# The small sums of A22 on VectorE behind the gates, and a wider order of the streams

## The chip, the cores and the metric

The kernel runs on one core of a Trainium2 chip. The metric is the device time of one execution in microseconds; the profiler's span of an execution goes from its first to its last instruction. TensorE does the matrix products, VectorE (DVE), ScalarE (ACT) and GpSimd (POOL) do the elementwise work, and SyncE (SP) issues most of the DMAs.

## The reference

A causal convolution of 7 taps per head over a sequence, with softmaxed weights, then a two-layer block with hardswish:

```python
out = np.einsum('hk,bskhg->bshg', softmax(weight), x_unf)     # x: 8 x 4096 x 192, 7 taps
x = out.reshape(32768, 192)
h = x @ w_in                                                  # 192 x 2048
g = h * np.clip(h + 3.0, 0.0, 6.0) / 6.0
return g @ w_out                                              # 2048 x 192
```

## The kernel before, in words

The tokens are worked through in 32 blocks of 1024, two halves of 512. The first block is done apart. For each of the blocks 1 to 31 the loop at the end of the kernel calls `first_layer` and then `second_layer`.

**First layer.** It has 16 units; `NP` is 8. Unit n multiplies one chunk of `w_in` (128 rows of the 2048) with the convolved block in three passes of exact float parts (18 matmuls, L437), into two banks of PSUM. Then `relu` (ACT, L311) and `gate` (VectorE, L315) make 128x1024 values of g. Gate n reads PSUM and the relu's result. Units 0 to 7 give the quarters A11 and A22 of g, units 8 to 15 the quarters A21 and A12. Four pairs of banks are used in turn, so unit n + 4 needs gate n to have read its banks. Behind the units stand other jobs: convolution taps of the next block on VectorE (L903; at n = 1, 5 and 9), sums for the second layer (`small_sums` on POOL for n below 8, L527; `g_sums`, L385, for S3 = A11 - A21 in pairs of chunks behind n = 9, 11, 13 and 15), and DMAs issued by POOL that add A22 onto A21 in place, which makes S1 (L506).

**Second layer.** The product with `w_out` is done as a 2x2 block product with 7 multiplications in place of 8 (Winograd's form). The sums S1 to S4 of g and T1 to T4 of the weights go into products 1 to 7. Three of the products (1, 4 and 5) have their last third of output columns done by the same scheme once more, on halves and quarters. These need small sums: `s1` for product 1, `s5` for product 5, and z1 to z4 of A22 for product 4:

z1 = x21 + x22, z2 = z1 - x11, z3 = x11 - x21, z4 = x12 - z2, where x11 to x22 are the quarters of A22.

TensorE's columns are used as four groups of 32, so four streams of matmuls run side by side. `plain`, `plain_half` and `small4` put matmuls into a stream; each has a place on a clock counted in units of 256 columns, and all four streams are 81 units long. `do(t, job)` puts a job of another engine at time t of that clock. All of it is sorted by clock and then recorded, and each engine runs its own instructions in that order. Partial sums wander from one stream's rows to another's by copies on ACT (L564), for example A4 to B4, B4 to C4, or e of one stream to e of the next; a VectorE sum (L405) takes some out into `p1` and `p4`.

The six banks are taken from units 12, 13 and 14 of the first layer: d and e from 12, b and c from 13, a and x_ from 14. `A4`, `E4`, `B4` and `C4` are parts of bank d; product 4's third output part `t4` is in b, product 1's third in b's fourth rows (V).

**What makes z1 to z4 before.** `s4_sums` in `first_layer`: ACT writes a seed, a copy of one quarter with a sign (L477), behind units 7 to 10; POOL then issues a DMA that adds another tensor onto it (`onto`, L480). z2 takes z1 and z4 takes z2 by such DMAs, so the third waits for the first, and the fourth for the third. In POOL's queue they stand between the S3 sums and the S1 DMAs. z3, z4 and their weights carry the opposite sign (`small_weights` with sign -1, and a fifth weight tile -b22).

**The last stage of a block.** `between` places the rounding of the next block's convolved values into high and low parts (`split_high` on ACT, L420; `split_rest` on VectorE, L423), the DMAs that swap their halves (`swap_parts`, SP), and the next load. The small sums s5 and the sums S2 and S4 (both `g_sums` with 4 chunks at a time) are on VectorE.

Of the kernel before, what the change touches and what calls it, by code (L numbers as in the profile page):

```python
# [31 lines left out]
def kernel(  # L32
# [30 lines left out]
    QS = 32  # L63
# [63 lines left out]
    w_out = cst.tile([P, NP, 7, DH], F32, name="w_out")  # L127
    B11, B12, B21, B22, T1, T2, T4 = range(7)
    T3 = B12
    w_s = cst.tile([P, 2, 4, NP // 2, QS], F32, name="w_s")  # L130
    w_s4 = cst.tile([P, 5, NP // 2, QS], F32, name="w_s4")

    w_in_bits = moe_w_in.bitcast(U32).rearrange("(p s) (c f w) -> c p s f w", s=K3, f=P, w=2)
    w_out_bits = moe_w_out.bitcast(U32).rearrange("(k c p) w -> p c k w", p=P, k=2)
# [240 lines left out]
    def g_sums(engine, which, slots, width):  # L375

        forms = {
            3: (S3, A11, A21, ALU.subtract),
            2: (S2, S1, A11, ALU.subtract), 4: (S3, A12, S2, ALU.subtract),
        }  # L380
        for n in which:
            o, a, b, op = forms[n]
            for p in slots[::width]:
                r = slice(p, p + width)
                engine.tensor_tensor(out=o[:, r], in0=a[:, r], in1=b[:, r], op=op)  # L385
# [18 lines left out]
    def add(out, x, y, op=ALU.add):  # L404
        nc.vector.tensor_tensor(out=out, in0=x, in1=y, op=op)  # L405
# [42 lines left out]
    def sums_a22():  # L448

        early = [  # L450
            part[:].rearrange("p s n -> p (s n)")[:, : NP * TH // 2]
            .rearrange("p (u t) -> p u t", t=TH)
            for part in z_early or y_own
        ]
        return early + [z[:, k] for k in range(2)]

    def first_layer(i, jobs):

        def unit(n):
            slot = free_slots.pop(0)  # L460
            for m_ in range(3):
                for s in range(K3):
                    products(n, slot, s, (m_,), s == 0, s == K3 - 1)
            to, both = places(n, slot)
            relu(to, both)
            gate(to, both)
            free_slots.append(slot)

        count = 2 * NP
        x11, x12, x21, x22 = four_parts(A22)  # L470

        def begin_sums():
            z_early[:] = own_tiles("z")
            seed(0, x21, 1.0)

        def seed(k, x, sign):
            nc.scalar.mul(sums_a22()[k], x, sign)  # L477

        def onto(k, x):
            nc.gpsimd.dma_start(out=sums_a22()[k], in_=x, accum_op=ALU.add)  # L480


        s4_sums = {
            NP - 1: [lambda: seed(2, x11, -1.0)],
            NP: [begin_sums, lambda: onto(2, x21), lambda: onto(0, x22)],
            NP + 1: [lambda: seed(1, x11, -1.0)],
            NP + 2: [lambda: seed(3, x12, -1.0), lambda: onto(1, sums_a22()[0])],
            NP + 6: [lambda: onto(3, sums_a22()[1])],
        }
        for job in jobs.get(-1, ()):  # L490
            job()
        for n in range(count):
            unit(n)
            for job in jobs.get(n, ()):
                job()
            for job in s4_sums.get(n, ()):
                job()
            if n == 1:
                s1.append(ot.tile([P, NP, N], F32, name="s1", tag="shared")[:])
            if n < NP and n % 2:  # L500
                small_sums(s1[-1], A11, (1, 2, 3, 4), nc.gpsimd, every[n - 1 : n + 1])
            if n > NP and n % 2:
                pair = slice(n - NP - 1, n - NP + 1)
                g_sums(nc.vector if n in (NP + 3, count - 1) else nc.gpsimd, (3,), range(NP)[pair], 2)
                if n + 3 < count:
                    nc.gpsimd.dma_start(out=S1[:, pair], in_=A22[:, pair], accum_op=ALU.add)  # L506
        for pair in (slice(NP - 2, NP), slice(NP - 4, NP - 2)):
            add(S1[:, pair], A21[:, pair], A22[:, pair])
# [4 lines left out]
    def four_parts(x):  # L513
        return [x[:, c::2, t] for t in halves for c in range(2)]
# [11 lines left out]
            o, p, q, op = forms[n]  # L526
            engine.tensor_tensor(out=o, in0=p, in1=q, op=op)  # L527

    def small_weights(to, w, sign=1):

        b11, b12, b21, b22 = (
            w_out[:, c::2, w, q * QS : (q + 1) * QS] for c in range(2) for q in range(2)
        )
        t1, t2, t3, t4 = (to[:, n] for n in range(4))
        third_sum = (t3, b22, b12) if sign > 0 else (t3, b12, b22)
        for o, p, q in ((t1, b12, b11), (t2, b22, t1), third_sum, (t4, b21, t2)):
            nc.gpsimd.tensor_tensor(out=o, in0=p, in1=q, op=ALU.subtract)
        if sign < 0:
            nc.scalar.mul(to[:, 4], b22, -1.0)

    def second_layer(i, between):
        last = i + 1 == NB
# [20 lines left out]
        def do(t, fn, *args, **kw):  # L563
            streams[3].append((t - 0.5, lambda: fn(*args, **kw)))  # L564
# [23 lines left out]
        def small(n, m_, out, start=False, j=3):  # L588

            x, w = prod[n]  # L590
            x11, x12, x21, x22 = four_parts(x)
            b11, b12, b21, b22 = (
                w_out[:, h::2, w, q * QS : (q + 1) * QS] for h in range(2) for q in range(2)
            )
            if n == 4:
                z1, z2, z3, z4 = sums_a22()
                t1, t2, t3, t4, b22 = (w_s4[:, k] for k in range(5))
            else:
                sums, ws = (s1[-1], w_s[:, 0]) if n == 1 else (s5, w_s[:, 1])
                z1, z2, z3, z4 = four_parts(sums)  # L600
                t1, t2, t3, t4 = (ws[:, k] for k in range(4))
            xm, wm = {
                1: (x11, b11), 2: (x12, b21), 3: (z4, b22), 4: (x22, t4),
                5: (z1, t1), 6: (z2, t2), 7: (z3, t3),
            }[m_]
            for u in range(NP // 2):
                put(j, 1, lambda u=u: matmul(
                    j, out[:, lo], wm[:, u], xm[:, u], start and u == 0
                ))
# [25 lines left out]
            do(clock[q], copy, out=e[rows(q + 1)] if q < 2 else p1[third], in_=e[rows(q)])  # L635

        plain(0, t4, 4, 2, (0,), True)
        plain_half(0, t4, 4, 2, 1, 0)
        do(clock[0], copy, out=t4[second], in_=t4[first])
        small4(0, 1, d[first], True)  # L640
        do(clock[0], copy, out=B4, in_=A4)
        small4(0, 2, d[first])
        do(clock[0], copy, out=p4[first, lo], in_=A4)
        plain_e(0)
        small4(0, 5, d[first, TH:], True)
        do(clock[0], copy, out=p4[second, lo], in_=E4)
        plain(0, c, 7, 0, every, True)

        plain(1, c, 7, 1, every[:3], True)
        for t, chunks in ((0, (2, 3, 4)), (1, (1, 2, 3, 4))):  # L650
            for ch in chunks:
                plain_half(1, t4, 4, 2, ch, t)
        do(clock[1], copy, out=t4[third], in_=t4[second])
        small4(1, 6, d[second])
        do(clock[1], copy, out=C4, in_=B4)
        plain_e(1)
        plain(1, c, 7, 1, every[3:6])
        small4(1, 3, d[second])
        do(clock[1] + 1, add, p4[second, lo], B4, p4[second, lo])
        plain(1, c, 7, 1, every[6:])  # L660

        plain(2, c, 7, 2, every, True)
        plain(2, t4, 4, 2, (5, 6, 7))
        do(clock[2], copy, out=p4[third], in_=t4[third])
        small4(2, 7, d[third])
        do(clock[2], add, p4[second, hi], C4, p4[second, lo])
        plain_e(2)
        plain(2, a, 2, 2, every[:2], True)
        small4(2, 4, d[third])
        do(clock[2], copy, out=p4[first, hi], in_=C4)  # L670
        plain(2, a, 2, 2, every[2:6])

        for q in range(NQ):
            if q < 2:
# [54 lines left out]

        for t, job in between:  # L730
            do(t, job)
        for t, n in ((22.3, 1), (30.7, 2), (30.7, 3)):
            do(t, small_sums, s5, S1, (n,), nc.vector)
        do(31, tiles)
        do(33, lambda: copy(out=late["p7"], in_=c[m]))
        do(37, copy, out=b[m], in_=p1[:])
        do(37, g_sums, nc.vector, (2,), every, 4)
        do(37, small_sums, s5, S1, (4,), nc.vector)
        do(37, g_sums, nc.vector, (4,), every, 4)
        do(61, lambda: add(late["u3"], b[m], late["p7"]))  # L740
        do(61, lambda: add(late["p7"], late["u3"], p4[:]))
        do(61, lambda: store(i, late["p7"], 1, 0))
# [69 lines left out]
    with tc.manual_schedule():  # L812
# [158 lines left out]

        def begin_block_two():
            w_sums(((T1, B12, B11), (T2, B22, T1), (T4, B21, T2)))
            for n, w in enumerate((B11, T1)):
                small_weights(w_s[:, n], w)
            small_weights(w_s4, T4, -1)
            conv.extend(conv_jobs(2))
            for job in conv[:3]:
                job()
# [20 lines left out]
        for i in range(1, NB):  # L1000
            jobs = {4 * n + 1: [job] for n, job in enumerate(conv[4:])}
            jobs[-1] = left + conv[3:4]
            first_layer(i, jobs)
            conv = []

            def begin_conv():
                x_tiles[i + 2] = load_x(i + 2)
                conv.extend(conv_jobs(i + 2))

            between = []  # L1010
            if i + 1 < NB:
                between = [(18, split_high), (20, split_rest), (23, swap_parts)]
            if i + 2 < NB:
                between += [(20, begin_conv), (60, lambda: conv[0]()), (72, lambda: conv[1]()), (73, lambda: conv[2]())]
            left = second_layer(i, between)
# [33 lines left out]
```

## Time and profile before

| | us |
|---|---|
| three runs | 2433.25, 2437.59, 2437.73 |
| median | 2437.59 |
| the profiled execution | 2436.49 |
| its span | 2434.7 |
| one steady block (1302.72 to 1378.04) | 75.32 |
| its first layer, units 0 to 7 and 8 to 15 | 16.90 and 16.43 |
| its second layer, to 1354.13 and after | 18.08 and 23.91 |

The columns of a timeline are start, length, engine, line, operation, output and inputs with their sizes, and a count where equal instructions were merged; brackets give the engine's idle time before the row and what ended it. A row of the chain of waits has start, length, engine, and what was worked on. The granted clock of TensorE was 0.997 of full speed over the whole span.

### The profile page before, as it was taken

Reading aid. Unit: us, or ns where it says so; the run is one execution under the profiler, and the core shown is the slowest. Engines: PE = TensorE matmul, PEld = TensorE weight load, DVE = VectorE, ACT = ScalarE, POOL = GpSimd, SP = SyncE. Lnnn points to the kernel's source line nnn. Section 1 sums busy time; section 2 is a strip of 40 time slices with the busy share of each in tenths; the row PEclk is TensorE's granted clock in tenths of the full one; section 3 lists DMA queues with packets and bytes.
Section 4 is the critical chain, followed back from the end, with each engine's and each line's share of the span. In section 5 each row is a group of like instructions: output and inputs, shape, how many; then the busy total and the mean of one; then the engine's idle time right before and its main releaser. Section 6 shows DMA issues by size and latency. Waiting matters only on the chain.

```text
span 2434.7 us, 52196 instructions
## 1 busy us (share of the span) xinstructions
PE 2330.1 (96%) x22652; PEld 1553.6 (64%) x22652; DVE 1959.7 (80%) x1681; ACT 1159.8 (48%) x1545; POOL 846.3 (35%) x803
## 2 busy tenths in 40 slices
PE   9999999999999999999999999999999999999998
PEld 5556666666675666766667656676566666666666
DVE  8877788887887888888878878788887878878866
ACT  7435545345443454434554445444455443454534
POOL 4513443134431344322443224432144332344323
PEclk9999999999999999999999999999999999999999
DMA  6355543455434554345543354533545435554344
GB/s 156 59 100 94 103 71 58 95 98 99 79 61 84 98 98 79 66 80 100 97 85 72 67 104 93 92 71 62 105 92 102 69 58 100 97 100 71 60 81 66
DMA packets 290774, 208.12 MB, mean 85 GB/s; under 512 B 209104, under 2 KB 245968, under 8 KB 290544
## 3 DMA queue, kind: packets, MB, share of 16 engines
q0 software_dynamic: 58912, 98.65, 24.9%
q1 hardware_dynamic: 230392, 105.86, 20.7%
q8 instruction: 177, 2.90, 0.5%
q14 instruction: 53, 0.43, 0.1%
q10 hardware_dynamic: 1240, 0.27, 0.1%
HBM read 31.72 MB, written 25.17 MB: 23 GB/s over the span
## 4 chain that ended last, share of the span: by engine, by line
PE 64%; POOL 13%; DMA 12%; ACT 5%; issue 3%; DVE 2%; POOLq 0%; ACTq 0%; DVEq 0%
PE psum L567 40%; PE psum L437 22%; DMA z<-g 12%; POOL s L527 7%; POOL s L385 3%; POOL z L480 2%; PE psum L326 2%; ACT psum L564 2%; POOL g L506 1%; ACT y L420 1%; DVE g L315 1%; ACT g L311 1%; DVE p L405 1%; ACT p L564 0%; ACT p L705 0%
## 5 line engine op out<-in xcount | busy, mean ns | idle before, releaser
L567 PE MATMUL psum<-g,w_out 128*32 128x512 f32 (+1 forms) x6526 | 1073.2, 519 | 40.6 <-ACT psum L564 40.6
L311 ACT ACTIVATE g<-psum,half 128x1024 f32<-128x1024 f32 x512 | 572.2, 1118 | 393.5 <-PE psum L437 393.3
L315 DVE SCALAR_TENSOR_TENSOR g<-g,psum 128x1024 f32<-128x1024 f32 x512 | 618.3, 1217 | 173.5 <-ACT g L311 169.3
L567 PE MATMUL psum<-s,w_out 128*32 128x256 f32 (+1 forms) x3272 | 717.2, 574 | 40.6 <-POOL s L385 40.6
L527 POOL TENSOR_TENSOR s<-g 128x256 f32<-128x256 f32 x248 | 267.5, 1079 | 1261.6 <-DVE g L315 969.0
L567 PEld LDWEIGHTS psum<-g,w_out 128*32 128x32 f32 x6526 | 395.2, 110 | 341.1 <-ACT psum L564 139.9
L437 PE MATMUL psum<-y,w_in 64*128 64x512 f32 x4608 | 548.4, 393 | 0.2
L437 PE MATMUL psum<-y_other,w_in 64*128 64x512 f32 x4608 | 530.1, 386 | 0.1
L437 PEld LDWEIGHTS psum<-y,w_in 64*128 64x128 f32 x4608 | 428.0, 184 | 134.9 <-issue 26.0
L437 PEld LDWEIGHTS psum<-y_other,w_in 64*128 64x128 f32 x4608 | 431.7, 184 | 92.7 <-DMA y_other<-y 0.5
L903 DVE SCALAR_TENSOR_TENSOR y<-x,c_sb,y 128x1536 f32<-128x1536 f32 x186 | 334.9, 1800 | 2.9 <-ACT y L901 1.8
L567 PEld LDWEIGHTS psum<-s,w_out 128*32 128x32 f32 x3272 | 231.6, 110 | 126.8 <-POOL s L385 54.6
L567 PE MATMUL psum<-g,w_s 128*32 128x256 f32 x1488 | 283.5, 379 | 0.0
L385 DVE TENSOR_TENSOR s<-g 128x1024 f32<-128x1024 f32 (+1 forms) x124 | 267.1, 2175 | 2.1
L385 POOL TENSOR_TENSOR s<-g 128x1024 f32<-128x1024 f32 x62 | 206.4, 3330 | 0.0
L564 ACT COPY psum<-psum 32x512 f32<-32x512 f32 (+1 forms) x217 | 106.3, 490 | 202.9 <-PE psum L567 200.5
L567 PE MATMUL psum<-z,w_s 128*32 128x256 f32 x992 | 178.8, 383 | 16.2 <-DVE p L405 16.0
L423 DVE TENSOR_TENSOR y<-y,y 128x1536 fp32r<-128x1536 f32 (+1 forms) x33 | 55.9, 1694 | 168.5 <-ACT y L420 168.5
L567 PE MATMUL psum<-s,w_s 128*32 128x256 f32 x744 | 181.5, 382 | 0.0
L567 PEld LDWEIGHTS psum<-g,w_s 128*32 128x32 f32 x1488 | 144.5, 110 | 50.4
L527 DVE TENSOR_TENSOR g<-g 128x1024 f32<-128x1024 f32 x124 | 148.6, 1219 | 5.4 <-PE psum L567 4.5
L385 DVE TENSOR_TENSOR g<-g 128x2048 f32<-128x2048 f32 x62 | 139.3, 2288 | 1.0
(94 smaller groups left out, 1627.4 us busy)
## 6 DMA issues: line engine op xcount, KB each, us to landing
y_other<-y SPq DMA_DIRECT2D x124, 384.0 KB, 5.7
z<-g POOLq DMA_DIRECT2D x62, 512.0 KB, 7.8
g<-g POOLq DMA_DIRECT2D x62, 512.0 KB, 8.1
z<-z POOLq DMA_DIRECT2D x62, 512.0 KB, 5.2
out_dram<-results SPq DMA_DIRECT2D x378, 64.0 KB, 2.0
x<-in_x_dram SPq DMA_DIRECT2D x53, 388.5 KB, 9.5
g<-in_moe_w_in_dram SPq DMA_DIRECT2D x16, 192.0 KB, 6.1
stage<-in_moe_w_out_dram SPq DMA_DIRECT2D x8, 384.0 KB, 6.2
```

The lines of the kernel that those rows point to most:

```text
L311: nc.scalar.activation(r6, h, ACT.Relu, bias=half[:], scale=1.0 / 6.0)
L315: nc.vector.scalar_tensor_tensor(out=g_, in0=g_, scalar=1.0, in1=h, op0=ALU.min, op1=ALU.mult)
L326: lambda p=p: nc.tensor.matmul(out=bank[j * QS : (j + 1) * QS, tokens], lhsT=w_out[:, p, w, cols], rhs=x[:, p, tokens], start=(first and p ...
L385: engine.tensor_tensor(out=o[:, r], in0=a[:, r], in1=b[:, r], op=op)
L405: nc.vector.tensor_tensor(out=out, in0=x, in1=y, op=op)
L423: engine.tensor_tensor(out=r32(out), in0=x, in1=high, op=ALU.subtract)
L437: nc.tensor.matmul(out=psum[:, 2 * slot + k], lhsT=r32(w_in_parts[wn][r, c, s]), rhs=r32(y_other[r, yn, s] if group else y_own[yn][r, s]), ...
L480: nc.gpsimd.dma_start(out=sums_a22()[k], in_=x, accum_op=ALU.add)
L527: engine.tensor_tensor(out=o, in0=p, in1=q, op=op)
L564: streams[3].append((t - 0.5, lambda: fn(*args, **kw)))
L567: nc.tensor.matmul(out=out, lhsT=w, rhs=x, start=start, stop=True, tile_position=(0, j * QS), skip_group_check=True,)
L903: jobs.append(lambda k=k: nc.vector.scalar_tensor_tensor(out=y[:], in0=x[:, :, k : k + N], scalar=c_sb[:, k : k + 1], in1=y[:], op0=ALU.mu ...
```

## The change

z1 to z4 are made by VectorE (`a22_sum`): each of the four sums is cut into two calls of two of the four chunks, and one call stands behind each of the units 8 to 15, in the order z1, z3, z2, z4. The ACT seeds and the four DMAs per block are gone, with the opposite signs. The S3 pair behind unit 11 goes from VectorE to POOL. In the second layer the streams are put in another order, and the jobs of other engines at other places on the clock.

```diff
         def begin_sums():
             z_early[:] = own_tiles("z")
-            seed(0, x21, 1.0)
-        def seed(k, x, sign):
-            nc.scalar.mul(sums_a22()[k], x, sign)
-        def onto(k, x):
-            nc.gpsimd.dma_start(out=sums_a22()[k], in_=x, accum_op=ALU.add)
-        s4_sums = {
-            NP - 1: [lambda: seed(2, x11, -1.0)],
-            NP: [begin_sums, lambda: onto(2, x21), lambda: onto(0, x22)],
-            NP + 1: [lambda: seed(1, x11, -1.0)],
-            NP + 2: [lambda: seed(3, x12, -1.0), lambda: onto(1, sums_a22()[0])],
-            NP + 6: [lambda: onto(3, sums_a22()[1])],
-        }
+        def a22_sum(n, u):
+            z1, z2, z3, z4 = sums_a22()
+            o, p, q, op = {
+                1: (z1, x21, x22, ALU.add), 2: (z2, z1, x11, ALU.subtract),
+                3: (z3, x11, x21, ALU.subtract), 4: (z4, x12, z2, ALU.subtract),
+            }[n]
+            add(o[:, u], p[:, u], q[:, u], op)
+        pairs = [slice(u, u + 2) for u in range(0, NP // 2, 2)]
+        s4_sums = {NP: [begin_sums]}
+        for k, (n_, u) in enumerate((n_, u) for n_ in (1, 3, 2, 4) for u in pairs):
+            s4_sums.setdefault(NP + k, []).append(lambda n_=n_, u=u: a22_sum(n_, u))
...
-                g_sums(nc.vector if n in (NP + 3, count - 1) else nc.gpsimd, (3,), range(NP)[pair], 2)
+                g_sums(nc.gpsimd if n + 1 < count else nc.vector, (3,), range(NP)[pair], 2)
...
         plain(0, t4, 4, 2, (0,), True)
-        plain_half(0, t4, 4, 2, 1, 0)
+        plain_half(0, t4, 4, 2, 2, 0)
...
-        plain_e(0)
         small4(0, 5, d[first, TH:], True)
         do(clock[0], copy, out=p4[second, lo], in_=E4)
+        plain_e(0)
         plain(0, c, 7, 0, every, True)
-        plain(1, c, 7, 1, every[:3], True)
-        for t, chunks in ((0, (2, 3, 4)), (1, (1, 2, 3, 4))):
-            for ch in chunks:
-                plain_half(1, t4, 4, 2, ch, t)
+        plain(1, c, 7, 1, every[:4], True)
+        plain_half(1, t4, 4, 2, 2, 1)
+        plain(1, t4, 4, 2, (1, 4, 6))
         do(clock[1], copy, out=t4[third], in_=t4[second])
         small4(1, 6, d[second])
         do(clock[1], copy, out=C4, in_=B4)
+        plain(1, c, 7, 1, every[4:6])
         plain_e(1)
-        plain(1, c, 7, 1, every[3:6])
         small4(1, 3, d[second])
-        do(clock[1] + 1, add, p4[second, lo], B4, p4[second, lo])
+        do(31.5, add, p4[second, lo], B4, p4[second, lo])
         plain(1, c, 7, 1, every[6:])
         plain(2, c, 7, 2, every, True)
-        plain(2, t4, 4, 2, (5, 6, 7))
+        plain(2, a, 2, 2, every[:2], True)
+        plain(2, t4, 4, 2, (3, 5, 7))
         do(clock[2], copy, out=p4[third], in_=t4[third])
         small4(2, 7, d[third])
         do(clock[2], add, p4[second, hi], C4, p4[second, lo])
         plain_e(2)
-        plain(2, a, 2, 2, every[:2], True)
+        plain(2, a, 2, 2, every[2:4])
         small4(2, 4, d[third])
         do(clock[2], copy, out=p4[first, hi], in_=C4)
-        plain(2, a, 2, 2, every[2:6])
+        plain(2, a, 2, 2, every[4:6])
...
-        for t, n in ((22.3, 1), (30.7, 2), (30.7, 3)):
+        for t, n in ((15.3, 1), (15.3, 3), (33.6, 2)):
             do(t, small_sums, s5, S1, (n,), nc.vector)
...
-        do(37, small_sums, s5, S1, (4,), nc.vector)
-        do(37, g_sums, nc.vector, (4,), every, 4)
+        do(42, small_sums, s5, S1, (4,), nc.vector)
+        do(42, g_sums, nc.vector, (4,), every, 4)
...
-                between = [(18, split_high), (20, split_rest), (23, swap_parts)]
+                between = [(21.2, split_high), (25.5, split_rest), (28, swap_parts)]
```

The weights of product 4's small level (`w_s4`, five tiles) become a third set of four in `w_s`, without the sign.

More of the change, by code (lines that the diff above doesn't have):

```diff
@@ L129 @@
     T3 = B12
-    w_s = cst.tile([P, 2, 4, NP // 2, QS], F32, name="w_s")
-    w_s4 = cst.tile([P, 5, NP // 2, QS], F32, name="w_s4")
+    w_s = cst.tile([P, 3, 4, NP // 2, QS], F32, name="w_s")
     w_in_bits = moe_w_in.bitcast(U32).rearrange("(p s) (c f w) -> c p s f w", s=K3, f=P, w=2)
@@ L452, in sums_a22 @@
             .rearrange("p (u t) -> p u t", t=TH)
-            for part in z_early or y_own
+            for part in z_early
         ]
@@ L527, in small_sums, with small_weights @@
             engine.tensor_tensor(out=o, in0=p, in1=q, op=op)
-    def small_weights(to, w, sign=1):
+    def small_weights(to, w):
         b11, b12, b21, b22 = (
@@ L534, in small_weights @@
         t1, t2, t3, t4 = (to[:, n] for n in range(4))
-        third_sum = (t3, b22, b12) if sign > 0 else (t3, b12, b22)
-        for o, p, q in ((t1, b12, b11), (t2, b22, t1), third_sum, (t4, b21, t2)):
+        for o, p, q in ((t1, b12, b11), (t2, b22, t1), (t3, b22, b12), (t4, b21, t2)):
             nc.gpsimd.tensor_tensor(out=o, in0=p, in1=q, op=ALU.subtract)
-        if sign < 0:
-            nc.scalar.mul(to[:, 4], b22, -1.0)
     def second_layer(i, between):
@@ L596, in small @@
                 z1, z2, z3, z4 = sums_a22()
-                t1, t2, t3, t4, b22 = (w_s4[:, k] for k in range(5))
             else:
-                sums, ws = (s1[-1], w_s[:, 0]) if n == 1 else (s5, w_s[:, 1])
-                z1, z2, z3, z4 = four_parts(sums)
-                t1, t2, t3, t4 = (ws[:, k] for k in range(4))
+                z1, z2, z3, z4 = four_parts(s1[-1] if n == 1 else s5)
+            t1, t2, t3, t4 = (w_s[:, (1, 5, 4).index(n), k] for k in range(4))
             xm, wm = {
@@ L973, in begin_block_two @@
             w_sums(((T1, B12, B11), (T2, B22, T1), (T4, B21, T2)))
-            for n, w in enumerate((B11, T1)):
+            for n, w in enumerate((B11, T1, T4)):
                 small_weights(w_s[:, n], w)
-            small_weights(w_s4, T4, -1)
             conv.extend(conv_jobs(2))
```

## The prediction

> **What bounds the kernel now.** I read the page first: TensorE is busy 96% of a 2434.7 us span at full clock, so only its idle time can be won or more of it lost. The chain of waits says who is on its path.
>
> ```profile
> span 2434.7 us, 52196 instructions
> PE 2330.1 (96%) x22652; PEld 1553.6 (64%) x22652; DVE 1959.7 (80%) x1681; ACT 1159.8 (48%) x1545; POOL 846.3 (35%) x803
> PE 64%; POOL 13%; DMA 12%; ACT 5%; issue 3%; DVE 2%; POOLq 0%; ACTq 0%; DVEq 0%
> ```
>
> A third of the chain is POOL, DMA, ACT and VectorE. One steady block runs from 1302.72 to 1378.04 us (75.3 us). First its chain in order of time (start, length, what):
>
> ```profile
> 1326.18 11.26 DMA z<-g
> ...
> 1338.02 0.90 POOL z L480
> 1338.91 1.23 POOL g L506
> 1340.14 2.39 POOL s L385
> ```
>
> POOL's queue stands at an accumulating DMA (L480, waiting 11.26 us for the one before), and S3's chunks 4 and 5 (L385) stand behind it. Then TensorE's timeline, with its weight loads (brackets: idle before, and what ended it):
>
> ```profile
> 1340.14 0.58 PEld L567 LDWEIGHTS psum<-g,w_out 128*32 128x32 f32 x8 [0.51 <-ACT psum L564]
> 1342.58 0.62 PE L567 MATMUL psum<-s,w_out 128*32 128x512 f32 x1 [1.38 <-POOL s L385]
> 1344.34 0.42 PE L567 MATMUL psum<-g,w_out 128*32 128x256 f32 x3 [0.71 <-ACT psum L564]
> 1351.27 0.62 PE L567 MATMUL psum<-g,w_out 128*32 128x256 f32 x2 [0.64 <-ACT psum L564]
> 1354.13 0.40 PE L567 MATMUL psum<-z,w_s 128*32 128x256 f32 x1 [0.51 <-DVE p L405]
> 1364.46 0.60 PE L567 MATMUL psum<-g,w_out 128*32 128x512 f32 x3
> 1364.89 0.60 PE L567 MATMUL psum<-g,w_out 128*32 128x512 f32 x3
> ```
>
> The last two rows give the pace: 0.43 us per unit of the code's clock. The second layer is 81 units, 34.8 us, and takes 42.0 (1336.05 to 1378.04): 7.1 us are stalls. Setting each row beside 1336.05 + 0.43 x its unit tells where: unit 7 is 1.1 us late (the copy A4 to B4), unit 8 3.1 (S3, so 2.0 more), unit 9 4.4 (the copy of V, 1.3 more), then 0.4 in small pieces, 1.4 at unit 21 (a copy behind split_high's 1.48 us on ACT), 0.9 about unit 26 (a VectorE sum behind split_rest). From 1354.13 nothing stalls. The first layer (33.4 us) has no stall.
>
> Now VectorE and POOL together, because the change moves work from DMA to VectorE where POOL is busy:
>
> ```profile
> 1317.91 1.81 DVE L903 SCALAR_TENSOR_TENSOR y<-x,c_sb,y 128x1536 f32<-128x1536 f32 x1
> 1327.95 2.43 DVE L315 SCALAR_TENSOR_TENSOR g<-g,psum 128x1024 f32<-128x1024 f32 x2
> 1339.83 4.92 DVE L405 TENSOR_TENSOR g<-g 128x1024 f32<-128x1024 f32 x2
> ```
>
> ```profile
> 1318.07 2.25 POOL L527 TENSOR_TENSOR s<-g 128x256 f32<-128x256 f32 x1 [0.47 <-DVE g L315]
> 1320.40 0.75 POOL L527 TENSOR_TENSOR s<-s,g 128x256 f32<-128x256 f32 x1
> 1326.95 3.48 POOL L385 TENSOR_TENSOR s<-g 128x1024 f32<-128x1024 f32 x1
> 1339.33 3.19 POOL L385 TENSOR_TENSOR s<-g 128x1024 f32<-128x1024 f32 x1
> ```
>
> The same POOL sum takes 0.75 alone and 2.25 when it starts under a convolution tap (L903): it ends 0.6 after the tap does. Two VectorE sums that should take 2.4 take 4.92: they end 2.2 after POOL's L385 does, at 1342.52. So a VectorE instruction with both inputs in SBUF and a POOL sum exclude each other. The gates (L315, one input in PSUM) run 1.21 each beneath POOL's L385 and are untouched. L385 itself needs 2.39 (the chain).
>
> **The change, part by part.** All times are in this block's frame, where gate n is ready at 1323.04 + 2.04 x (n - 8).
>
> Removed: four ACT seeds (4 x 1.06) and four POOL DMA issues. ACT idles 0.9 between gates, so the seeds were free; the DMAs' price is the 2.0 at unit 8. Five of the 31 blocks are 1.2 to 2.7 us longer than the rest, where the same DMA came later still (12.55 instead of 11.1 in the chain); that is 9 us in all and goes too.
>
> Added: eight VectorE sums of 512 elements, about 0.65 each (0.69 for the 96x512 sums of L405, with overlap), one behind each of gates 8 to 15 (sum 1 behind gate 8). One S3 sum of 2 chunks goes from VectorE to POOL (n = 11), so POOL has three of 2.39, each released by gates 9, 11 and 13. Alone, gate plus sum is 1.22 + 0.65 = 1.87 of the 2.04 period and would hide. But every L385 shuts the sums out, and a sum waiting in VectorE's queue holds the gates behind it. Step by step: gate 8 ends 1324.26; sum 1 waits for a POOL sum of the pair before and ends 1325.4; gate 9 1326.6; the tap of n = 9 1328.3. Now L385 (asked for at 1326.7) and sum 2 both want to run. I let POOL go first: it was there first, as at 1339.33, where L385 was issued before L405 and won. L385 to 1330.7, sum 2 to 1331.35, gate 10 to 1332.5 (before: 1329.2), sum 3 to 1333.1, gate 11 to 1334.3. Sum 4 follows its gate at once and goes first, 1334.9; L385 to 1337.3; gate 12 beneath it; sum 5 waits, 1337.95; gate 13 ends at 1339.1 (before: 1334.5).
>
> All four streams of the second layer start in the banks of unit 13 (b and c), and the built program has its first matmul wait for that gate. So it starts at 1339.1 and not at 1336.05: **3.05 us per block**. The rest fits: S3's chunks 4 and 5 are ready 3.1 us after that start (sum 6, then L385) and needed at 4.5; chunks 6 and 7 at 6.8, needed at 8.3; the last of A22's sums at 5.6, needed at unit 25; behind L385 POOL has nothing left to do.
>
> If VectorE goes first after the tap, the same steps end gate 13 at 1337.95, a delay of 1.9; if sum 1 also waits for the whole POOL pair, 3.7. I take 3.05.
>
> The Trainium skill, "SBUF — State Buffer", Who interferes with whom, says that issue order decides who holds the port pair shared by VectorE and GpSimd, and that the other blocks for the whole instruction. By that rule POOL goes first here too, and the sum stays at 3.05 instead of 1.9; the trace's one such meeting had another POOL instruction in front, so it is not a clean test.
>
> Second layer: same 81 units (two half matmuls become one whole; rows of 388 and 594 at the same pace). Gone: 2.0 (unit 8), 1.4 (unit 21, split_high now comes after those copies), 0.9, and 0.2 of the small ones: 4.5. Kept: units 7 and 9. New, because the built program waits by bank and not by stream: E4 now comes straight behind A4 in bank d and waits for A4's copy (unit 11; price of unit 7 above its baseline, 0.8); B4 straight behind E4, and e0 two units behind A (unit 15: 0.7); a's second chunk at unit 18 waits for the copy of E (0.5); C4 at unit 29 waits for VectorE's p1 sum, which stands behind split_rest (1.76): 1.1; C4's last product at unit 37 right behind C's copy (0.9). New: 4.0, bounds 3.0 to 5.0 by these rows. **Net -0.5 us per block.** The moved VectorE sums s5 and S2 land before units 45, 53, 61 and 65 with 1.4 us or more left; swap_parts five units later on SP's queue still has 30 us until y_other is read. The weights at the start (one ACT negation of 0.31 less) are nothing.
>
> **Sum:** 31 x (3.05 - 0.5) - 9 = +70 us on the profiled execution's 2436.5 us: **2506 us**. That execution is 1.1 us under the shown median, 2437.59, so no correction is made.
>
> **Rivals.** (a) *Faster: gates are not late.* Place: the exclusion after gates 9 to 13; it decides if gate 13 ends less than 0.8 us after 1336.05 (0.8 = 0.5 + 9/31). For it: 1.87 of 2.04 fits, and S3's wait on the DMA is truly gone. Against it: the 4.92 row. Time: 31 x -0.5 - 9 = -24, 2412 us; with the new stalls at their low bound 2381. (b) *VectorE first after the tap:* delay 1.9, +34, 2471 us. For it: VectorE issues its next instruction just before the last ends. (c) *The bank waits are the worse part:* new stalls of 5.0 (net +0.5) and a delay of 3.7: 31 x 4.2 - 9 = +121, 2558 us. (d) *The change does nothing that can be told:* delay near 0.8, 2437 us; it needs two prices to cancel.
>
> **How the numbers follow.** Forecast 0.55, (b) 0.13, (c) 0.07, all slower: 0.75. (a) 0.20; (d) 0.05, within 0.2% (5 us, about the spread of the three runs). Range 2410 to 2550: from (a)'s own time to just short of (c); below lies part of (a), above half of (c). Slower alone: 2465 to 2550.
>
> **What would show it.** The gates' line should have its last four gates 2 to 6 us behind their ACT partners; the sums of z on VectorE a mean near 1.4 us instead of 0.69; the first matmul of each second layer about 2.5 to 3 us idle, ended by the gate. S3 should vanish from TensorE's releasers, DMA z from the chain, and copies should show at units 11, 15, 18 and 37. Wrong if the z sums last 0.7 and that first gap is under 0.8 us; or if the gap is there and the second layer lasts under 40 us.

## The result, and the profile after

The changed kernel takes **2477.65 us** (median of four runs, 2474.94 to 2480.51). The kernel before, run beside it, takes 2437.66 (2433.25 to 2438.28). The ratio is 1.0168, 95% interval 1.015 to 1.0186: slower by 40 us, where 2506 was forecast. The page of the profiled execution (2476.09 us) has the same rows as before: span, busy times, and the chain of waits by engine.

```profile
span 2474.3 us, 51699 instructions
PE 2348.4 (95%) x22466; PEld 1528.2 (62%) x22466; DVE 2111.4 (85%) x1898; ACT 1044.5 (42%) x1420; POOL 867.9 (35%) x710
PE 72%; DVE 19%; ACT 5%; issue 3%; POOL 0%; DMA 0%; ACTq 0%; DVEq 0%
```

DMA and POOL, a quarter of the chain before, have left it. VectorE has gone from 2% to 19%. Cutting the timeline at the first matmul of each layer shows where the 40 us arise. These are medians over the blocks, worked out from the starts of TensorE's rows:

| kernel | first layer's start to second's | second layer | block |
|---|---|---|---|
| before | 33.33 | 41.87 | 75.20 |
| after | 35.72 | 40.80 | 76.52 |

So in the median block the second layer starts 2.39 us later and lasts 1.07 less. Added up over the 31 blocks, the first layers are 71.5 us longer (the last block, which has no taps of a next one, is not late) and the second layers 31.9 shorter: 39.6, the whole difference of the two profiled executions. VectorE's timeline of the steady block that starts at 1014.92 shows the delay arise (start, length, engine, line, operation, tiles and sizes; brackets give idle time before and what ended it):

```profile
1037.44 1.21 DVE L314 SCALAR_TENSOR_TENSOR g<-g,psum 128x1024 f32<-128x1024 f32 x1
1038.57 1.80 DVE L894 SCALAR_TENSOR_TENSOR y<-x,c_sb,y 128x1536 f32<-128x1536 f32 x1
1040.30 2.88 DVE L404 TENSOR_TENSOR z<-g 128x512 f32<-128x512 f32 x1
1043.10 1.21 DVE L314 SCALAR_TENSOR_TENSOR g<-g,psum 128x1024 f32<-128x1024 f32 x1
1044.23 0.68 DVE L404 TENSOR_TENSOR z<-g 128x512 f32<-128x512 f32 x1
...
1047.70 1.75 DVE L404 TENSOR_TENSOR z<-z,g 128x512 f32<-128x512 f32 x1
1049.38 1.21 DVE L314 SCALAR_TENSOR_TENSOR g<-g,psum 128x1024 f32<-128x1024 f32 x1
```

POOL's timeline of the same stretch:

```profile
1038.72 3.90 POOL L384 TENSOR_TENSOR s<-g 128x1024 f32<-128x1024 f32 x1 [0.60 <-DVE g L314]
...
1046.13 2.77 POOL L384 TENSOR_TENSOR s<-g 128x1024 f32<-128x1024 f32 x1 [2.00 <-DVE g L314]
```

S3's sum (L384) is recorded from 1038.72, under the tap (L894), and ends at 1042.63, 2.26 behind the tap's end at 1040.37, which is about the length that it needs. The sum of z, recorded from 1040.30, ends 0.55 later. Gate 10 (1043.10) waits behind it. The second S3 sum, 1046.13 to 1048.90, holds up the sum recorded from 1047.70 in the same way, and with it gate 13, which ends at 1050.59.

The second layer then starts. These are rows of TensorE's weight loads:

```profile
1050.64 0.11 PEld L560 LDWEIGHTS psum<-g,w_out 128*32 128x32 f32 x1 [2.31 <-DVE g L314]
...
1054.73 0.12 PEld L560 LDWEIGHTS psum<-g,w_out 128*32 128x32 f32 x2 [0.51 <-ACT psum L557]
...
1056.53 0.12 PEld L560 LDWEIGHTS psum<-g,w_out 128*32 128x32 f32 x3 [0.80 <-ACT psum L557]
...
1058.11 0.11 PEld L560 LDWEIGHTS psum<-z,w_s 128*32 128x32 f32 x1 [1.01 <-ACT p L557]
```

The first gap, 2.31 us, is ended by the gate. The next two rows wait for the copies A4 to B4 (unit 7) and V to e (unit 9), the last for the copy of A4 into p4: it is the first product into E4 (unit 11). Later in the same second layer the chain in order of time has:

```profile
1064.45 1.50 ACT y L419
1065.97 1.76 DVE y L422
1067.76 0.44 DVE p L404
1068.24 3.67 PE psum L560 x20
1071.92 0.02 issue
1071.94 0.37 ACT p L699
```

ScalarE's split (L419), VectorE's rest of it (L422) and, behind that, the sum of C into p1 end the stall at unit 29; a copy (L699) ends the one at unit 37. After that nothing stalls, as in the kernel before.

### The profile page after: what moved, and what is told of

It is laid out like the page before. It is cut to its first block, busy times and chain, and to the rows that moved or that the text cites. A ratio compares the mean times of both kernels' runs of the same rounds, so it can differ in the third digit from the quotient of the medians.

```text
span 2474.3 us, 51699 instructions
## 1 busy us (share of the span) xinstructions
PE 2348.4 (95%) x22466; PEld 1528.2 (62%) x22466; DVE 2111.4 (85%) x1898; ACT 1044.5 (42%) x1420; POOL 867.9 (35%) x710
## 4 chain that ended last, share of the span: by engine, by line
PE 72%; DVE 19%; ACT 5%; issue 3%; POOL 0%; DMA 0%; ACTq 0%; DVEq 0%
PE psum L560 44%; PE psum L436 25%; DVE z L404 8%; DVE g L314 6%; DVE y L422 2%; DVE y L894 2%; ACT y L419 2%; PE psum L325 2%; ACT g L310 2%; ACT psum L557 1%; DVE p L404 1%; ACT p L699 0%; ACT p L557 0%; PE psum L818 0%; PE psum L826 0%
## 5 line engine op out<-in xcount | busy, mean ns | idle before, releaser
L560 PE MATMUL psum<-s,w_out 128*32 128x256 f32 (+1 forms) x3272 | 729.9, 576 | 0.0
L560 PEld LDWEIGHTS psum<-g,w_out 128*32 128x32 f32 x6340 | 379.3, 109 | 359.6 <-DVE g L314 69.3
L436 PE MATMUL psum<-y_other,w_in 64*128 64x512 f32 x4608 | 539.5, 388 | 3.3
L560 PE MATMUL psum<-g,w_s 128*32 128x256 f32 x1488 | 342.1, 380 | 13.5 <-ACT p L699 13.5
L894 DVE SCALAR_TENSOR_TENSOR y<-x,c_sb,y 128x1536 f32<-128x1536 f32 x186 | 335.0, 1801 | 2.3 <-ACT y L892 1.2
L384 POOL TENSOR_TENSOR s<-g 128x1024 f32<-128x1024 f32 x93 | 291.4, 3133 | 86.3 <-DVE g L314 86.3
L560 PEld LDWEIGHTS psum<-g,w_s 128*32 128x32 f32 x1488 | 161.0, 110 | 89.1 <-ACT p L699 29.4
L557 ACT COPY psum<-psum 32x512 f32<-32x512 f32 (+1 forms) x217 | 106.3, 490 | 181.3 <-PE psum L560 179.0
L384 DVE TENSOR_TENSOR s<-g 128x2048 f32<-128x2048 f32 (+1 forms) x93 | 176.7, 1927 | 0.0
L404 DVE TENSOR_TENSOR z<-g 128x512 f32<-128x512 f32 x124 | 164.6, 1327 | 0.0
L560 PEld LDWEIGHTS psum<-z,w_s 128*32 128x32 f32 x744 | 74.2, 109 | 127.9 <-ACT p L557 48.9
```

What stands on the lines that cost most here:

```text
L436: nc.tensor.matmul(out=psum[:, 2 * slot + k], lhsT=r32(w_in_parts[wn][r, c, s]), rhs=r32(y_other[r, yn, s] if group else y_own[yn][r, s]), ...
L560: nc.tensor.matmul(out=out, lhsT=w, rhs=x, start=start, stop=True, tile_position=(0, j * QS), skip_group_check=True,)
L894: jobs.append(lambda k=k: nc.vector.scalar_tensor_tensor(out=y[:], in0=x[:, :, k : k + N], scalar=c_sb[:, k : k + 1], in1=y[:], op0=ALU.mu ...
```

## The experiments

Each kernel is the changed one with the edit shown, unless said otherwise. Each was profiled once except where a ratio is given; the kernel before ran beside them at 2436.55, 2433.33 and 2430.26 us in the three groups of single runs. "Block" is from one first layer's start to the next. The theory that they try has two separate costs and one gain. The costs are late gates, because VectorE's sums of z and POOL's S3 sums shut each other out, and a stream order with stalls of its own. The gain is that S3 no longer stands behind the accumulating DMAs. A row's lateness is how far it starts behind the second layer's start + 0.43 us x its unit.

**Second input from PSUM.** The sums of z take their second input from a bank of PSUM, so z1 to z4 and what is made of them have other values than the reference's; all the work is still there:

```
-            add(o[:, u], p[:, u], q[:, u], op)
+            s = 2 * free_slots[-1]
+            add(o[:, u], p[:, u], psum[:, s : s + 2, 0:TH], op)
```

> From the changed kernel; the second input of each small sum of A22 is read from PSUM instead of SBUF (so z1 to z4 are not the reference's sums; all else is computed). Theory (a VectorE instruction with two SBUF inputs and a POOL instruction exclude each other, and sums that wait hold up the gates): with one SBUF input the sums no longer wait; their mean falls from 1.27 to about 0.7 us, the first matmul of a second layer follows the first layer without the 1.9 us gap, and the span falls by 31 x 2.4 = 74 us to about 2400. Rival (VectorE simply has too much to do behind gates 8 to 15): the sums are as many and as long, the gap stays, 2474.

Measured: 2401.77 us, span 2400.0, block 33.35 + 40.84 = 74.19. The delay of 2.39 is gone to 0.02 and nothing else moved. The groups of instructions (line, engine, operation, tiles and sizes, count, busy us, mean ns, idle before) show the sums at their own length, with as many POOL sums as before:

```profile
L384 POOL TENSOR_TENSOR s<-g 128x1024 f32<-128x1024 f32 x93 | 291.2, 3132 | 29.4 <-DVE g L314 29.4
L404 DVE TENSOR_TENSOR z<-g,psum 128x512 f32<-128x512 f32 x186 | 126.9, 682 | 0.0
```

The changed kernel has for its first 124:

```profile
L404 DVE TENSOR_TENSOR z<-g 128x512 f32<-128x512 f32 x124 | 164.6, 1327 | 0.0
```

With as many sums on VectorE and as many on POOL the delay is gone, so it comes of the two SBUF inputs.

**S3 all on VectorE.** POOL has no S3 sum left beneath the late gates:

```
-                g_sums(nc.gpsimd if n + 1 < count else nc.vector, (3,), range(NP)[pair], 2)
+                g_sums(nc.vector, (3,), range(NP)[pair], 2)
```

> From the changed kernel; the S3 pairs of n = 9, 11 and 13 go from POOL to VectorE, so POOL has nothing to run beside the small sums of A22 after its sums for s1. Theory (exclusion): VectorE gets three sums of 1.2 us more but loses the waits; gate 13 ends about 1.3 us late instead of 2.4; span about 2474 - 34 = 2440. Rival (VectorE overfull): 3 x 1.2 us more ahead of gate 13 (two of them), gap grows to 4 us or more, 2530 or more.

Measured: 2443.52 us, span 2441.6, block 34.72 + 40.84 = 75.57. The delay falls from 2.39 to 1.39: what is left is VectorE's own load, with S3 at 1.22 us a call, and one meeting a block with POOL's `s1` sums: the first 124 sums of z still have a mean of 0.79 us and not 0.68. The gap before the second layer falls from 1.88 to 1.30 us.

**Old streams.** The three streams of product 4, the s5 sums and the places of the split are those of before; the sums and S3 stay changed:

```
+        plain_e(0)
         small4(0, 5, d[first, TH:], True)
         do(clock[0], copy, out=p4[second, lo], in_=E4)
-        plain_e(0)
...
-        plain(2, a, 2, 2, every[:2], True)
-        plain(2, t4, 4, 2, (3, 5, 7))
+        plain(2, t4, 4, 2, (5, 6, 7))
...
-                between = [(21.2, split_high), (25.5, split_rest), (28, swap_parts)]
+                between = [(18, split_high), (20, split_rest), (23, swap_parts)]
```

> From the changed kernel; the streams, s5 sums and split_high/split_rest stand where they stood before the change, the sums of A22 stay on VectorE. Theory (the order of the streams by itself costs, since copies and sums are waited for by bank; the gain of the second layer is S3's wait on the DMA, 2.0 us, and nothing else): second layer 7.15 - 2.0 = 5.15 us of stalls instead of 6.0, span 2474 - 28 = 2447. Rival (the new order brings the 1.0 us that the second layer became shorter): without it the second layer is back at 41.9, span 2474 + 31 = 2505.

Measured: 2434.57 us, span 2432.8, block 35.71 + 39.51 = 75.23, better than theory and rival. Timed again, with what was expected of it:

> Timed again: the changed kernel with the streams and places of before (A22's sums on VectorE and one S3 sum more on POOL are then the whole change). Theory (the late gates cost per block what S3's wait for the DMA gave back): a ratio to the kernel before of 0.998 to 1.001. Rival (the profiled executions differ by chance, and the sums by themselves cost or gain something that can be told): a ratio outside 0.995 to 1.005.

2433.70 us against 2438.72, ratio 0.9982 (0.9973 to 0.999). VectorE's sums, with one S3 pair more on POOL, thus cost next to nothing: they take 2.38 us per block in late gates and give back 41.87 - 39.51 = 2.36 in the second layer, where S3 is no longer late. This kernel's chain in order of time shows the stalls of before that remain at units 21 to 22:

```profile
1119.25 0.37 ACT p L696
1119.62 0.02 issue
1119.64 1.18 ACT y L419
1120.82 0.33 issue
1121.15 0.56 ACT psum L557
```

TensorE waits for a copy (L557) that stands behind the split (L419) on ScalarE.

**New streams, old sums.** The kernel before with the changed kernel's streams and places (the last diff, the other way round); ACT seeds and POOL DMAs are kept.

> From the kernel before; only the order of the streams and the places of s5, split_high and split_rest are the changed kernel's, the sums of A22 stay ACT seeds and POOL DMAs. Theory: no late gate; second layer 6.0 us of stalls plus 2.0 at unit 8 for S3 behind the DMA, 42.8 us: span 2435 + 31 x 0.9 = 2463. Rival (the new order is a gain of 1.0 us or more per block): 2435 - 31 = 2404 or less.

Measured: 2481.27 us, span 2479.4, block 33.34 + 43.19 = 76.53. Against before the order costs 1.32 us per second layer; with the changed sums (last experiment to after) it costs 40.80 - 39.51 = 1.29. Theory and rival were both too low in time: the theory's 2463 is 0.9 per block. Eight blocks of 76.9 to 79.8 us add to it here. With the old sums or the new, the order alone costs about as much as the whole change loses.

**Old streams and S3 on VectorE**, the second and third edits together.

> The changed kernel with both repairs at once: the stream order of before, and all of S3 on VectorE. Theory (two separate costs that add up): from one first layer's start to the second layer's 34.7 us, as with S3 on VectorE alone, and 39.5 us for the second layer, as with the old order alone: 74.2 us per block, a span of about 2401 us (2432.8 less 31 x 1.0). Rival (the second layer of the old order only looked short because its start was late, so that what comes from VectorE is late relative to an earlier start): the block stays near 75.2 us and the span above 2425.

Measured: 2401.47 us, span 2399.6, block 34.72 + 39.51 = 74.23. The two add up to the hundredth.

**Spread sums.** On top of the last: only four half calls stay among the gates, and sums 3 and 4 go behind S3's last chunks:

```
-        for k, (n_, u) in enumerate((n_, u) for n_ in (1, 3, 2, 4) for u in pairs):
-            s4_sums.setdefault(NP + k, []).append(lambda n_=n_, u=u: a22_sum(n_, u))
+        for k, n_, u in ((0, 1, 0), (2, 1, 1), (5, 2, 0), (6, 2, 1)):
+            s4_sums.setdefault(NP + k, []).append(lambda n_=n_, u=u: a22_sum(n_, pairs[u]))
...
+        for n_ in (3, 4):
+            a22_sum(n_, slice(0, NP // 2))
         for pair in (slice(NP - 2, NP), slice(NP - 4, NP - 2)):
```

> The kernel of the last experiment with A22's small sums spread: two halves of sum 1 behind gates 8 and 10, two halves of sum 2 behind gates 13 and 14, sums 3 and 4 in whole calls of 1.22 us behind the last S3 sum. Theory (gate 13 is late by just what stands before it on VectorE; three of the sums of 0.65 are no longer there, and VectorE has 0.4 us to spare in each pair of gates): start to start 33.4 to 33.7 us, second layer 39.5, block 72.9 to 73.2, span 2360 to 2370 us. Rival (sums 3 and 4 and what stands behind them on VectorE now come too late for the second layer, and it gives the gain back): second layer 40.5 us or more, span 2395 or more.

Measured: 2359.77 us, span 2357.9, block 33.33 + 39.51 = 72.84. The delay is gone altogether, and the later sums cost nothing.

**Spread sums, later split.** The last kernel with the split at 21.2, 25.5 and 28.

> The kernel of the last experiment with the changed kernel's later places for the split of y (21.2, 25.5, 28 instead of 18, 20, 23). Theory (the stalls of 1.6 us at units 21 to 22 and 0.95 at unit 26 are copies that stand behind the split on ScalarE and a sum that stands behind its rest on VectorE, and nothing takes their place): second layer 37.0 us, span about 2285 us. Rival (the split finds other copies and sums to stand before, wherever it is put): second layer 38.7 to 40 us, span 2340 to 2380.

Measured: 2372.82 us, span 2371.0, second layer 39.94. The theory fell. By their lateness, unit 22 is better (2.89 us behind instead of 3.73), but unit 26 is worse (4.92 instead of 4.50): the rest of the split then stands ahead of B4's sum on VectorE, a stall of 2.2 instead of 0.95. The rival is right in kind; its time of 2340 to 2380 holds.

**E4 behind plain_e(0).** In the changed kernel, this one step of stream 0 as before:

```
+        plain_e(0)
         small4(0, 5, d[first, TH:], True)
         do(clock[0], copy, out=p4[second, lo], in_=E4)
-        plain_e(0)
```

> The changed kernel with one step of stream 0 put back: chunk 5 of product 1 (plain_e of 0) before the small product 5 into E4 instead of behind it. Theory (E4's first matmul at unit 11 waits for the copy of A4 in the same bank, 0.9 us, and is two units later now): that stall goes, and the second layer lasts 39.9 to 40.2 us, span about 2450 us. Rival (a wait by bank only moves: the chunk into bank e meets the product of A and its copies there): second layer 40.6 to 41.2, span within 8 us of 2474.

Measured: 2441.28 us, span 2439.5, second layer 39.71, 1.09 less. The wait of E4's first matmul at unit 11 is gone: it was 2.74 us behind there, and no row of units 11 and 12 is now more than 2.31. By unit 18 the same row of stream 2 is 2.68 behind instead of 3.70. One misplaced step is four fifths of what the order costs.

**Early split.** The changed kernel with the split's places of before (18, 20, 23).

> The changed kernel with the places of the split of y, its rest and the swap put back to those of before (18, 20, 23). Theory (the 1.2 us at unit 29 is VectorE's sum into p1 standing behind the rest of the split, and the new stream order leaves enough units between the copies and their use at units 18 to 25 for the split to hide there): the stall at unit 29 goes and none of before's stalls at units 21, 22 and 26 comes back; second layer 39.5 to 39.8 us, span 2434 to 2443. Rival (the copies behind the split are late again, whatever the order): 1.4 us or more at units 21 to 26; second layer 41 us or more, span 2480 or more.

Measured: 2456.68 us, span 2454.9, second layer 40.09. No stall came back at units 21 to 26, as the theory has it, but the one at unit 29 went only from 1.2 to 0.5: the split's rest makes 0.7 of it, and the rest is there without the split. Theory and rival both miss the time.

**Combined.** S3 on VectorE, spread sums, `plain_e(0)` ahead of E4 and the early split in one kernel.

> The changed kernel with four edits together: S3 all on VectorE, A22's sums spread over gates 8, 10, 13, 14 and behind the last S3 sum, chunk 5 of product 1 before E4, and the split at before's places. Theory (each cost found so far is separate: start to start 33.3 us as with the spread sums, second layer 40.8 less 1.1 for E4 less 1.2 for the split, 38.5): block 71.8, span about 2327. Rival (the stall of one place is taken over by the next, here by sums 3 and 4 that come 2 to 3 us later than in the changed kernel, or by the copies behind the split): second layer 39.5 us or more, span 2357 or more.

Measured: 2348.14 us, span 2346.3, block 33.35 + 39.08 = 72.43, against 2430.26 for the kernel before on the same chip: 82 us less, in one profiled execution. The two single prices of the second layer give 40.80 - 1.09 - 0.71 = 39.00; the theory's 38.5 rested on 1.2 for the split. This is the fastest of the kernels run.

**C4 moved away from C.** The combined kernel with C4's product 7 at unit 33 and product 4 at unit 41:

```
+        plain_e(2)
+        plain(2, a, 2, 2, every[2:4])
         small4(2, 7, d[third])
         do(clock[2], add, p4[second, hi], C4, p4[second, lo])
-        plain_e(2)
-        plain(2, a, 2, 2, every[2:4])
+        plain(2, a, 2, 2, every[4:6])
         small4(2, 4, d[third])
         do(clock[2], copy, out=p4[first, hi], in_=C4)
-        plain(2, a, 2, 2, every[4:6])
...
-        do(31.5, add, p4[second, lo], B4, p4[second, lo])
+        do(37.3, add, p4[second, lo], B4, p4[second, lo])
```

> The kernel with the four edits together, and C4's two products moved in stream 2: product 7 from unit 26 to unit 33, product 4 from unit 37 to unit 41, so that neither is written while VectorE or ScalarE reads level two's part C in the same bank d; the sum of B4 into p4 goes behind that of C4. Theory (the stalls of 0.7 us at unit 29 and 1.0 at unit 37 are waits for those readers of bank d): both go, second layer 37.3 to 37.8 us, span 2298 to 2315, ratio to before 0.945 to 0.952. Rival (they are waits for something else, or come back where C4 is now written, since e's third part and C4's sum are later now): second layer 38.6 us or more, span 2331 or more, ratio 0.958 or more.

Measured: 2577.80 us, ratio 1.0569 (1.0555 to 1.0582), block 33.34 + 46.42 = 79.77. In this kernel sum 4 of s5 overwrites A22's last quarter at 41.5, and three of product 4's four matmuls read it after that, so it computes other values than the reference's; only its waits are read here. Both stalls in question did go: from unit 29 to unit 40 the lateness stays between 3.5 and 4.3 us, with no step at 29 or 37. But 1.2 us appear at unit 26, and unit 41 waits twice. The first of unit 41's waits in the chain in order of time:

```profile
1186.41 4.49 DVE g L384 x2
1190.91 0.03 issue
1190.94 0.43 DVE p L404
```

B4's sum into p4, put at 37.3, stands behind S2's two sums on VectorE, and bank d is not free until it has been read; then product 4 waits for s5's sum 4 (1.23 us). So the bank reading is borne out at unit 37. At unit 29 it is not shown, since 1.2 us lost at unit 26 are enough to cover a wait of 0.7 behind them. The placement was bad, and a version without these faults was not run.

## Why the prediction was right, and where its sizes were off

**The direction and the two mechanisms that carry the sum were right; a third term, the long blocks, had mostly the wrong cause.** POOL went first after the tap, as chosen against rival (b). The Trainium skill, "SBUF — State Buffer", Who interferes with whom, says that two SBUF inputs contend with GpSimd's reads and that issue order decides who blocks; the trace agrees: L384 was recorded 1.6 us ahead of the sum of z (1038.72 and 1040.30), and the sum ended 0.55 behind it. With one input in PSUM the sums took 0.68.

**The delay, 3.05, measured 2.39.** The steps came in the order written, each a little shorter. From the block's start, the first S3 sum was forecast to end at 27.98 and ended at 27.71; gate 10 at 29.78, 29.39; the second S3 sum at 34.58, 33.98; gate 13 at 36.38, 35.67. Each S3 sum ended 2.25 or 2.26 us after what it waited for, where 2.39 was the chain's part of a row of 3.19 that stood behind a DMA issue (1340.14 to 1342.52), and the sum of z behind it 0.55 later instead of 0.65: 0.24 twice. Another 0.15 was there by gate 9, and the remaining gates and sums came at a pitch of 1.13 and 0.60, since an instruction starts 0.08 before the last one ends. This is 30 x 0.66 = 20 us of the miss, and 3 more are the last block, which was counted among 31 and is not late.

**The second layer, -0.5, measured -1.07.** By its parts this was -2.0 for S3 and +1.5 for the order (4.0 new, 2.5 gone), and the runs give -2.36 and +1.29. S3's lateness was under-sized by 0.36: part of unit 9's old step of 1.3, put down to the copy of V and kept, was S3 as well; that unit costs 0.75 to 0.9 by itself. The new stalls came where they were named, 3.45 in all: unit 11 0.9 (0.8 forecast), unit 15 0.5 (0.7), unit 18 0.2 (0.5), unit 29 1.2 (1.1), unit 37 0.65 (0.9). In the last two blocks S3 is not late even in the kernel before: their second layers take 39.52 and 44.28 us there and 40.80 and 45.56 in the changed kernel, 1.28 more each, the order's price with nothing won. So the miss is 29 x 0.57 = 16.5 us one way and 2 x 1.78 = 3.6 the other.

**The long blocks, -9.** Three blocks of 77.8 to 78.4 us remain among the changed kernel's. Over their own median they hold 4.7 us, where five hold 9.0 in the kernel before: 4.4 us were won, not 9. The prediction put all five down to a later DMA. The trace shows that DMA late in two of them (12.55 and 12.39 us in the chain), but in four of them TensorE's granted clock stands at 0.50 for 3.41 us, from the stalls at units 8 and 9 on. It does so in just the three long blocks of the changed kernel, behind the first gap (the rows are in the last section), so this part was not the DMA's to give back. In the six experiments whose clock never falls within a block, no block is more than 0.3 us over the median.

The sizes add up: 20 and 3 for the gates, 16.5 - 3.6 for the second layer and -4.6 here are 31, against the 30 between 2506 and the profiled execution's 2476.

**What the sum hid.** The prediction put the late gates at +3.05 and the second layer at nearly nothing, and so reads as if the gates made the kernel slower. By the runs they eat S3's gain (2.38 against 2.36), and the loss is as large as the order's price; the +1.5 stood in the list of stalls but was never drawn out as a sum of its own. Of what was named to show each step, the last four gates (3.2 to 4.0 us behind their ACT partners), the absence of S3 and of the DMA from the chain, and the copies are there as written. The first gap (2.31 us for 2.5 to 3) and the first sums of z (a mean of 1.33, the others 1.21 and 1.22, for 1.4) are there and a little smaller.

## What to carry to other kernels

Sums moved from a DMA to VectorE were cheap here only where no POOL sum with two SBUF inputs ran beneath: give them an input in PSUM (74 us here, with other values), keep POOL's sums out of that stretch (33 us), and don't put them ahead of the gate that starts the next stage (both together 75 us on the old streams). A distance of so many units between a partial sum and its use has to be kept per bank and not per stream, since one step that broke it in bank d cost 1.1 us a block. Before a long instruction is moved, list what stands behind it on its engine at the new place: the later split won 0.8 us at unit 22 and lost 1.3 at unit 26. And keep stalls of TensorE short: one of 1.3 us a block never cost its clock here, one of 1.9 sometimes did.

## What the runs showed of the hardware

**A stall of 1.9 us can halve TensorE's clock.** In the last experiment's second layer TensorE's matmuls stood for 3.36 us, and the granted clock went to 0.50. The table by stretches has its bounds, its length, busy time and instructions of TensorE, its weight loads, VectorE, ScalarE and POOL, then the clock, the DMA share and GB/s:

```profile
1183.00:1187.00 4.00, 4.00 (x54) 2.37 (x50) 2.69 (x5) 1.20 (x4) 0.00 (x0) 1.00 0.71 164
1187.00:1191.00 4.00, 1.05 (x11) 0.14 (x3) 3.97 (x3) 0.75 (x2) 0.00 (x0) 0.91 0.00 0
1191.00:1195.00 4.00, 3.13 (x13) 0.77 (x16) 2.85 (x3) 0.00 (x0) 0.00 (x0) 0.50 0.00 0
1195.00:1199.00 4.00, 4.00 (x40) 2.07 (x37) 3.14 (x2) 0.68 (x2) 0.00 (x0) 0.74 0.00 0
```

The idle time ends at 1191.41 (4.25 us for the weight loads); a matmul of 128x512 then took 1.06 us instead of 0.60, and the clock is back at 1.00 by 1197.9. The changed kernel's gap before the second layer is much shorter, 1.86 to 1.91 us in 30 blocks (2.28 to 2.33 for the loads), and mostly, as in the block shown above, the clock stayed at 1.00. In three blocks it did not. One of them, with its gap, the stretch behind it and the next (the columns as before):

```profile
358.56:360.46 1.90, 0.00 (x1) 0.00 (x1) 1.90 (x3) 1.11 (x1) 1.36 (x2) 1.00 0.00 0
360.72:364.14 3.42, 3.42 (x22) 1.20 (x16) 3.42 (x4) 0.20 (x1) 2.51 (x1) 0.50 0.89 153
364.14:367.50 3.36, 3.36 (x30) 1.11 (x24) 3.33 (x4) 0.94 (x3) 0.00 (x0) 1.00 0.00 0
```

The other two half-rate stretches start at 1203.82 and 1818.21. From start to start that is 247.0 and 180.0 times 3.413 us, so they fit a window that runs on whatever the kernel does. The Trainium skill, "TensorE: Matmul & The Clock Gate", What's actually happening, gives a half-rate state after an idle window of about 3.4 us; here 1.9 us of idle time were enough in three blocks of 30. Gaps of 1.30 us, in the kernel with S3 on VectorE, were never followed by it. Why the same gap halves the clock in one block and not in the next is not shown.

**VectorE's sum waits behind a POOL DMA issue, too.** In the kernel before, VectorE's last S3 sum of the first layer took 4.90 us in one block and 1.23 in another. VectorE's rows of the two:

```profile
1113.03 4.90 DVE L385 TENSOR_TENSOR s<-g 128x1024 f32<-128x1024 f32 x1
...
1338.57 1.23 DVE L385 TENSOR_TENSOR s<-g 128x1024 f32<-128x1024 f32 x1
```

and POOL's of the two:

```profile
1112.92 1.54 POOL L506 DMA_DIRECT2D g<-g  x1
1113.65 3.19 POOL L385 TENSOR_TENSOR s<-g 128x1024 f32<-128x1024 f32 x1
...
1338.60 1.54 POOL L506 DMA_DIRECT2D g<-g  x1
1339.33 3.19 POOL L385 TENSOR_TENSOR s<-g 128x1024 f32<-128x1024 f32 x1
```

Recorded 0.11 us after the DMA's issue, the sum waits for it and for the POOL sum that follows, and ends at 1117.93, 1.09 behind the latter; recorded 0.03 before, it runs at once. All blocks with this DMA agree: the 14 sums recorded behind its issue, by 0.04 to 0.35 us, take 4.67 to 4.97 us, the 15 recorded ahead of it 1.22 or 1.23. The order was not changed in an experiment of its own.
